# Attention and MLP on one core: transfers cut along other dimensions, first queries turned by TensorE, four chunks' residuals on ScalarE and GpSimd, and new instruction orders

## The chip, the core and the metric

The kernel runs on one core of a Trainium2 chip. Its time is the device time of one execution in microseconds (us). A core has five engines with a queue each, which run in order and wait for each other by semaphores: TensorE (PE; its weight loads are shown as PEld), VectorE (DVE), ScalarE (ACT), GpSimd (POOL) and SyncE (SP). Transfers are issued from the queues of SP and ACT here (one from POOL) and are moved by 16 DMA engines.

## What is computed

Two blocks follow each other. The first is attention with a polynomial sketch, without a softmax: with batch 4, 4 heads, 1088 tokens, head size 32 and r = 8,

```python
def phi(x):
    a = np.einsum('rd,bhsd->bhsr', S1, x)
    b = np.einsum('rd,bhsd->bhsr', S2, x)
    return np.einsum('bhsi,bhsj->bhsij', a, b).reshape(*x.shape[:-1], r * r)
q_p, k_p = (phi(q), phi(k))
kv = np.einsum('bhsf,bhsd->bhfd', k_p, v)
z = np.sum(k_p, axis=2)
num = np.einsum('bhsf,bhfd->bhsd', q_p, kv)
den = np.einsum('bhsf,bhf->bhs', q_p, z)[..., None] + 1e-06
attn = num / den
```

The heads are then put side by side, x of shape (4, 1088, 128), and the second block is

```python
xn = (x - mu) / np.sqrt(var + 1e-06) * g_ln
out = x + np.maximum(xn @ w_ch1, 0.0) @ w_ch2
```

with 512 hidden columns. S1, S2 and both weights come as float64; the kernel makes float32 of them with integer and float operations on their two words.

## The kernel before, in words

**Stages of a batch.** A batch's k and q are loaded (`ld`) and turned by DVE in blocks of 32 x 32 (`turn_g`, `turn_r`), so that head and feature lie on the partitions. For batch 0, `k_dir` and `q_dir` make the features on PE straight with tokens on the partitions; for the others `k_feat` and `q_feat` make them in packed 32-row matmuls and DVE turns them (`k_tok`, `q_tok`). `k_prod` and `q_prod` make the 64 products per token (POOL or DVE). `k_sum`, `k_zs`, `k_sc`, `k_sccp` give the denominator's vector, `k_val`, `k_vcp`, `k_spr`, `k_rcp` the value matrix. `q_ac`, `q_den`, `q_rec`, `q_a2` divide, `q_turn` turns the products, and `num` (PE) gives x, turned, in PSUM; `num_cp` and `num_r` copy it to SBUF.

**Chunks.** x is worked on in eight chunks of 512 tokens (0 to 7, two for each batch) and two of 128 (8 and 9, the last 64 tokens of two batches each). For a chunk, `hid` (PE, one of four blocks of hidden columns) and `relu` make the hidden layer, `sec` (PE, one of four 128-token tiles, 8 matmuls) the second product; the normalisation is put into w1 (`fold`) and, as a factor rstd, behind the second product. x itself is also needed with tokens on the partitions ("rows"): for mean and variance (`st_bn`, `st_ag`, then `st_pow` on POOL for the power -0.5) and for the residual. Chunks 0, 1, 8 and 9 get their rows by PE (`row_pe`, `row_cp`); chunks 2 to 7 by way of DRAM: `row_turn` on DVE, `row_wr` (a store to a scratch tile) and four `row_rd` (loads back, one for each head). `fin` (DVE) scales by rstd and adds the rows, into one of two buffers `ob`, and `store` sends the chunk.

**What sets the order.** Nothing is scheduled: a string `PROGRAM` lists the operations by name, engine letter (V, A, G, S) and arguments, and each engine gets its instructions in the order of this list. At most eight transfers of SP and ACT are under way together: their eight semaphores go round, and an issue waits for the eighth before it. PSUM has the banks X and Y (two tiles of 1024 columns each, for `num` and the features), M, N, O and K; `hid` uses M and N, `sec` mostly O.

**Lines.** `ld_v` 132-138, `ld_vr` 141, `row_turn` 692, `row_wr` 696, `row_rd` 701, `st_bn` 708, `st_ag` 713 (line 717 is the addition of 1e-6), `hid` 732, `relu` 738, `sec` 747, `fin` 761, `store` 782, `store_r` 791. Line 85 is the helper for elementwise products, line 80 that for ACT copies. The shapes of the transfers that the change touches are these (step and count of each dimension, DRAM side):

```python
# ld_v:   [[8 * D, 4], [G * D, 32], [1, 8 * D]]   into 128 partitions, one head
# row_wr: [[P, P], [P * P, 4], [1, P]]            from 128 partitions
# row_rd: [[P * P, 4], [P, 32], [1, P]]           into 128 partitions, one head
# store:  [[8 * DM, 4], [G * DM, 32], [1, 512]]   from 128 partitions
```

Of the kernel before, what the change touches and what calls it, by code (L numbers as in the profile page):

```python
# [25 lines left out]
def kernel(  # L26
# [44 lines left out]
    banks = {"X": XS[0], "Y": XS[1], "M": M[0], "N": M[1], "O": PO, "K": KV}  # L71
# [26 lines left out]
    qn = const([P, G * D], F32, "qn", B)  # L98
# [67 lines left out]
    mhalf = const([P, 4], F32, "mhalf")  # L166
    m896 = const([P, 1], F32, "m896")
# [249 lines left out]
    @op  # L417
    def turn_r(x, b):
        dst, src = turned[x]
        o = 1024 + 64 * (b % 2)  # L420
        dve.transpose(dst[b % 2][:, o : o + 64], src[b][:, 1024:1088])
# [8 lines left out]
    @op  # L430
    def k_dir(u0, u1, z):
        for u in range(u0, u1):
            pe.matmul(banks[z][:, KW * (u - u0) : KW * (u - u0 + 1)], kT[0][:, P * u : P * (u + 1)],
                      sk0, start=True, stop=True)
# [228 lines left out]
    xh = const([P, 512], F32, "xh", 2)  # L663
    xd = [dram.tile([P, 512], F32, name=f"xd{i}") for i in range(8)]
# [5 lines left out]
    obs = const([P, 512], F32, "ob", 2)  # L670
# [42 lines left out]
    def st_ag(c):  # L713
        n, st, mv = tiles(c), sts[slot(c)], mvs[slot(c)]
        for t in range(n):
            dve.bn_aggr(out=mv[:, 2 * t : 2 * t + 2], in_=st[:, 6 * t : 6 * t + 6])
        dve.tensor_scalar(out=vas[slot(c)][:, 0:n], in0=_ap(mv, 0, P, 1, [[2, n]]), scalar1=1e-6,  # L717
                          scalar2=None, op0=ALU.add)
# [42 lines left out]
    def fin(z, c, t):  # L761
        o, i0 = halves(c, obs[turn_of(c)][:, P * t : P * (t + 1)], banks[z][:, P * t : P * (t + 1)])
# [28 lines left out]
    def store_r(eng, c, i):
        b = 2 * (c - 8) + i
        by[eng].dma_start(
            out=bass.AP(out.tensor, out.offset + (b * S + 32) * DM,
                        [[DM, 2], [G * DM, 32], [1, DM]]),
            in_=obs[turn_of(c)][64 * i : 64 * i + 64, 0:P],
# [5 lines left out]
    ld_s A 0; ld_g; ld S k 0 0 16; c_small; c_ones; ld_s A 1; ld S k 0 16 34; c_iota;  # L802
    ld_u S q 0 0 4; c_act; c_pads 0; c_masks; ld_w S 1; c_vpad 3; c_vpad 2; ld_v S 0 0; c_rest;
    ld_v S 0 1; c_vpad 0; ld_v S 0 2; c_ac 0; c_vpad 1; w_ex V 0 0 64; c_ac 1; ld_v S 0 3;
    c_ident; w_exf V 0 0 64; w_e2 V 0 0 64; ld_vr S 0 0; w_bits V 0 0 64; turn_g k 0 0 2;
    w_mant A 0 0 64; c_pads 1; ld_vr S 0 1; w_addlow V 0 0 64; w_e3 V 0 0 64; s_heads V;
    turn_g k 0 2 4; fill 2 512; fill 1 256; sk; ld_u S q 0 4 8; turn_u q 0 0 4; sk_q; sk_2;
    sk_qq 2; sk_8; sk_0; sk_qq 3; sk_d; turn_r k 0; fill 1 256; fill 1 128; k_dir 0 3 X; c_cg V;
# [6 lines left out]
    q_dir 0 4 N; w_e3 V 1 0 256; ld_vr S 1 0; w_add G 1 256 512; turn_r q 0; turn_u q 0 4 8;
    k_val 0; w_e3 V 1 256 512; q_cp A 0 4 N 16 24; q_ac0 0 4 N 0; w_add G 1 0 256; q_den 0 0 4;
    q_rec 0 0 4; ld_vr S 1 1; w_low A 2 0 512; q_dir 4 9 O; w_mul G 1 0 256; q_b0 0 4 N 0;
    k_vcp A 0; q_prod0 0 2 N 0; w_mul G 1 256 512; q_prod0 2 4 N 0; k_spr 0; q_cp A 4 9 O 16 24;
    q_turn 0 2; k_rcp A 0; fold N 0 256; ld S k 2 0 34; turn_g k 1 0 4; num 0 0 2;
    fold_cp A N 0 256; turn_r k 1; num_cp A 0 0 0 2; q_turn 2 4; num_cp A 0 1 0 2; hid M 0 0 0 2;  # L820
    q_ac0 4 9 O 4; q_den 0 4 9; ld S q 2 0 34; hid N 0 1 0 2; q_rec 0 4 9; relu A M 0 0 0 2;
    turn_r q 1; ld_v S 2 0; num 0 2 4; q_b0 4 9 O 4; relu A N 0 1 0 2; q_prod0 4 9 O 4;
    ld_v S 2 1; fold M 256 512; ld_v S 2 2; num_cp A 0 1 2 4; num_cp A 0 0 2 4; ld_v S 2 3;
    row_pe 0 K; fold_cp A M 256 512; q_turn 4 9; ld_vr S 2 0; row_cp A 0 K; hid N 0 2 0 2;
    ld_vr S 2 1; hid M 0 3 0 2; relu A N 0 2 0 2; w_bits V 2 0 512; relu A M 0 3 0 2; num 0 4 9;
    turn_g q 1 0 4; w_mant A 2 0 512; ld S k 3 0 34; w_add G 2 0 512; hid M 0 1 2 4; turn_r k 2;
    num_r A 0; turn_g k 2 0 4; num_cp A 0 0 4 8; num_cp A 0 1 4 8; k_feat 1; relu A M 0 1 2 4;
    w_ex V 2 0 512; row_pe 1 K; ld S q 3 0 34; k_tok 1; w_exf A 2 0 512; hid M 0 3 2 4;
    ld_v S 3 0; turn_r q 2; row_cp A 1 K; k_prod G 1 5 9; w_e2 V 2 0 512; hid N 0 0 2 4;
    ld_v S 3 1; relu A M 0 3 2 4; st_bn 1; k_sum 1; relu A N 0 0 2 4; ld_v S 3 2; hid M 1 1 0 4;  # L830
    k_zs 1; turn_g q 2 0 4; ld_v S 3 3; ld_vr S 3 0; k_prod G 1 0 5; k_sc 1; ld_vr S 3 1;
    hid N 0 2 2 4; relu A M 1 1 0 4; k_sccp V 1; st_bn 0; q_feat 1; relu A N 0 2 2 4; st_ag 0;
    hid N 1 0 0 4; w_e3 V 2 0 512; k_val 1; st_pow 0; turn_r k 3; relu A N 1 0 0 4; q_tok 1 0;
    turn_g k 3 0 4; w_mul G 2 0 512; hid N 1 2 0 4; k_vcp A 1; turn_r q 3; q_tok 1 1; sec O 0 3;
    relu A N 1 2 0 4; q_ac V 1 0 4; q_den 1 0 4; sec O 0 2; q_ac V 1 4 9; q_rec 1 0 4; st_ag 1;
    q_a2 G 1 0 4; turn_g q 3 0 4; sec O 0 1; q_prod G 1 0 4; sec O 0 0; q_den 1 4 9; q_rec 1 4 9;
    hid M 1 3 0 4; fin O 0 0; fin O 0 1; q_a2 G 1 4 9; fin O 0 3; fin O 0 2; k_feat 2; q_turn 0 4;
# [76 lines left out]
```

## Time and profile before

| What | Value |
|---|---|
| Runs | 139.17, 141.32, 141.88 us; median 141.32 |
| Profiled execution, span | 139.2 us |
| Busy: PE, DVE, POOL, ACT | 105.5, 75.8, 49.4, 39.6 us |
| Mean granted TensorE clock | 0.89 |
| DMA | 13.32 MB in 14023 packets, mean 96 GB/s |

The profiled execution's span is taken by the profiler from the first to the last instruction. In the profile, a busy row gives the share of each of 40 equal slices in tenths (9 is 90% or more); the clock row gives the TensorE clock that was granted; the DMA row gives the mean busy share of the 16 DMA engines. A group or timeline row names line, engine, operation, output<-inputs, shape and count, and in brackets the idle time in front of it and what ended that. Matmul times overlap each other, since matmuls are pipelined.

### The profile page before, as it was taken

To read this page: it belongs to the slowest core of one execution; us is meant where nothing else is said; L and a number is where in the kernel's file an instruction comes from. 1 tells how busy PE (TensorE), PEld (TensorE's weight loads), DVE (VectorE), ACT (ScalarE), POOL (GpSimd) and SP (SyncE) were. 2 spreads that over 40 slices of the span, in tenths; PEclk is the share of its full clock that TensorE was granted. 3 is DMA by queue.
4 is the path that set the end of the run, shared out by engine and by line. 5 is a ranking of instruction groups with operands and counts; after the bars stand their busy time and mean duration, and the time that the engine had idled before them with its cause. 6 is when DMAs were issued, how large, how long until landed. Compare 5 with 4: busy or idle time off the path is not lost.

```text
span 139.2 us, 3266 instructions
## 1 busy us (share of the span) xinstructions
PE 105.5 (76%) x1336; PEld 72.0 (52%) x1336; DVE 75.8 (54%) x225; ACT 39.6 (28%) x99; POOL 49.4 (36%) x62
## 2 busy tenths in 40 slices
PE   5998598999986899999105999907999999970000
PEld 2486565764483865493003785403779467970000
DVE  4897499879599839400994307079434400038110
ACT  4055143486211132604200505104114443210000
POOL 6329300039917992610667600047800100005000
PEclk9999855699999999999975799996899999999555
DMA  4849939528532115223002052221002612210220
GB/s 137 238 132 227 315 111 245 158 101 235 177 99 68 16 64 151 57 79 77 24 0 56 19 153 66 78 87 26 0 0 37 196 30 66 82 49 0 36 102 31
DMA packets 14023, 13.32 MB, mean 96 GB/s; under 512 B 1848, under 2 KB 11832, under 8 KB 14008
## 3 DMA queue, kind: packets, MB, share of 16 engines
q1 hardware_dynamic: 13812, 13.04, 33.1%
q8 instruction: 10, 0.16, 0.5%
q10 hardware_dynamic: 164, 0.07, 0.2%
q14 instruction: 5, 0.04, 0.1%
q0 software_dynamic: 32, 0.00, 0.0%
HBM read 9.31 MB, written 3.80 MB: 94 GB/s over the span
## 4 chain that ended last, share of the span: by engine, by line
DMA 46%; SPq 16%; DVE 14%; PE 10%; POOL 4%; issue 3%; ACT 3%; DVEq 0%; ACTq 0%
DMA vn<-in_v_dram 15%; DMA x<-xd 12%; DMA xd<-xh 9%; SPq L702 9%; DMA kn<-in_k_dram 5%; DMA out_dram<-ob 4%; PE X L633 4%; SPq L133 3%; POOL qp L85 3%; DVE st L710 3%; PE M L734 3%; DVE qpT L619 3%; PE PO L750 3%; ACT xT L80 2%; DVE xh L693 2%
## 5 line engine op out<-in xcount | busy, mean ns | idle before, releaser
L734 PE MATMUL M<-xT,w 128*128 128x512 f32 (+1 forms) x72 | 34.8, 604 | 5.0 <-ACT hT L742 4.6
L742 ACT ACTIVATE hT<-M 128x512 f32<-128x512 f32 (+2 forms) x44 | 21.4, 500 | 36.5 <-PE M L734 30.1
L750 PEld LDWEIGHTS PO<-w,hT 128*128 128x128 f32 x208 | 25.1, 194 | 7.0 <-DVE ob L763 3.2
L750 PE MATMUL PO<-w,hT 128*128 128x128 f32 x208 | 26.4, 279 | 1.9 <-DVE ob L763 1.4
L723 POOL TENSOR_TENSOR rstd<-va,mhalf 128x4 f32<-128x4 f32 (+1 forms) x10 | 9.6, 957 | 48.7 <-DVE va L717 48.5
L710 DVE BATCH_NORM_STATS2 st<-x 128x6 f32<-128x128 f32 x32 | 7.0, 280 | 27.1 <-DMA x<-xd 27.0
L734 PEld LDWEIGHTS M<-xT,w 128*128 128x128 f32 x72 | 12.3, 201 | 15.2 <-ACT hT L742 10.3
L85 POOL TENSOR_TENSOR kp<-kf 128x1024 f32<-128x1024 f32 (+3 forms) x8 | 15.2, 1916 | 3.6 <-ACT kf L80 2.2
L85 POOL TENSOR_TENSOR qp<-a,fq 128x1024 f32<-128x1024 f32 (+1 forms) x6 | 13.0, 2171 | 0.4
L619 DVE STREAM_TRANSPOSE qpT<-qp 128x1280 f32<-128x1280 f32 (+2 forms) x9 | 11.1, 1228 | 2.5 <-POOL qp L85 2.4
L80 ACT COPY xT<-X 128x256 f32<-128x256 f32 (+1 forms) x18 | 5.4, 361 | 17.3 <-PE X L633 17.3
L633 PE MATMUL X<-qpT,kvr 32*32 32x288 f32 (+2 forms) x384 | 9.4, 404 | 0.3 <-DVE qpT L619 0.3
L750 PEld LDWEIGHTS X<-w,hT 128*128 128x128 f32 x64 | 7.8, 192 | 1.4 <-issue 1.4
L237 PE MATMUL M<-ones 128*128 128x256 f32 (+2 forms) x16 | 7.2, 574 | 1.5 <-DVE ones L181 1.5
L750 PE MATMUL X<-w,hT 128*128 128x128 f32 x64 | 8.0, 275 | 0.0
L475 PE MATMUL KV<-kf 128*32 128x32 f32 x72 | 1.7, 212 | 8.0 <-DVE kf L460 8.0
L763 DVE SCALAR_TENSOR_TENSOR ob<-PO,rstd,x 128x128 f32<-128x128 f32 x24 | 6.7, 337 | 1.8 <-PE PO L750 1.8
L633 PEld LDWEIGHTS X<-qpT,kvr 32*32 32x32 f32 x384 | 5.2, 119 | 3.6 <-issue 2.1
L305 POOL TENSOR_TENSOR mant<-mant,low 128x256 f32<-128x256 f32 (+1 forms) x3 | 2.9, 988 | 11.5 <-ACT mant L283 11.5
L581 DVE STREAM_TRANSPOSE fq<-X 128x576 f32<-128x576 f32 x6 | 4.4, 754 | 4.1 <-PE X L572 4.1
L504 PE MATMUL KV<-kp,vn 128*32 128x64 f32 x288 | 5.1, 221 | 1.2 <-DMA vn<-in_v_dram 1.1
L475 PEld LDWEIGHTS KV<-kf 128*32 128x32 f32 x72 | 1.2, 121 | 9.1 <-DVE kf L460 8.2
(115 smaller groups left out, 123.7 us busy)
## 6 DMA issues: line engine op xcount, KB each, us to landing
vn<-in_v_dram SPq DMA_DIRECT2D x16, 128.0 KB
out_dram<-ob SPq DMA_DIRECT2D x8, 256.0 KB
kn<-in_k_dram SPq DMA_DIRECT2D x3, 544.0 KB
qn<-in_q_dram SPq DMA_DIRECT2D x3, 544.0 KB
xd<-xh SPq DMA_DIRECT2D x6, 256.0 KB
x<-xd SPq DMA_DIRECT2D x24, 64.0 KB
w_raw<-in_moe_w_ch_dram SPq DMA_DIRECT2D x2, 512.0 KB
qn<-in_q_dram SPq DMA_DIRECT2D x2, 256.0 KB
```

The source lines that it names most:

```text
L80: act.copy(o, i)
L85: by[eng].tensor_tensor(out=o, in0=a, in1=b, op=ALU.mult)
L237: pe.matmul(M[0][:, 0:w], ones[:, 0:P], ones[:, 0:w], start=True, stop=True)
L619: dve.transpose(_ap(qpT, 0, P, 32 * u0, [[32, u1 - u0], [TW, 8], [1, 32]]), qp[:, H * F * u0 : H * F * u1])
L633: pe.matmul(XS[r // 2][D * h : D * h + D, o : o + w], kvr[b % 2][rows, DM * f + D * h : DM * f + D * h + D], qpT[rows, c : c + w], start=( ...
L702: by[eng].dma_start(out=rows_of(c)[:, P * h : P * (h + 1)], in_=bass.AP(xd[c].tensor, xd[c].offset + 32 * P * h, [[P * P, 4], [P, 32], [1, ...
L710: dve.bn_stats(out=sts[slot(c)][:, 6 * t : 6 * t + 6], in_=row_ap(c, t))
L723: pool.tensor_tensor(out=rstds[slot(c)][:, 0:n], in0=vas[slot(c)][:, 0:n], in1=mhalf[:, 0:n], op=ALU.pow)
L734: pe.matmul(banks[z][:, 0:n], w1[:, P * j : P * (j + 1)], cols(c)[:, a : a + n], start=True, stop=True)
L742: act.activation(o, i, AF.Relu)
L750: pe.matmul(banks[z][:, DM * t : DM * (t + 1)], h[:, 512 * j + P * t : 512 * j + P * (t + 1)], w2[:, DM * j : DM * (j + 1)], start=(j == 0 ...
L763: dve.scalar_tensor_tensor(out=o, in0=i0, scalar=rstds[slot(c)][:, t : t + 1], in1=row_ap(c, t), op0=ALU.mult, op1=ALU.add)
```

## The change

What it does:

1. **Transfers with 32 or 128 outer runs.** `ld_v` takes all heads of 32 partitions (8 tokens each) in place of one head in all 128; `row_wr` and `row_rd` write and read a chunk whole, with 128 runs, one read in place of four; `store` has 128 runs for batch 0 and 32 x 4 for the others. To fit, `num_cp`, `row_turn` and `turn_r` place the tokens in another order, and w1 and w2 are loaded in parts.
2. **First queries.** Batch 0's q is loaded with tokens on the partitions (`ld_t`, `ld_tr`: pieces of 32 floats, 128 bytes) and turned by PE (`turn_p`, nine transposes) and copied by ACT (`turn_c`), in place of `ld_u` and DVE's `turn_u`.
3. **Residuals.** Chunks 0, 1, 2 and 3 use `fin_a` (ACT scales the product by rstd into `ob`) and `fin_g` (POOL adds the rows) in place of `fin`. There are four `ob` buffers in place of two.
4. **Smaller ones.** Batch 1's k uses `k_dir` as batch 0 does. The 1e-6 in `st_ag` comes from a tile (`tensor_tensor`) in place of a constant (`tensor_scalar`). The halves of X and Y are banks of their own (A to D), and `hid` and `sec` use all of them. Some relus, PSUM copies, products and all of w2's unpacking but one step are on DVE.
5. **Orders.** The list `PROGRAM` is another one. Rows of chunks 4 and 5 are read from ACT's queue (`row_rd A 5`, `row_rd A 4`, behind `relu A D 4 3`), the others from SP's; chunk 7 goes to DRAM and back ahead of chunk 6; in front of the first `num` now stand both batches' `k_dir` and `k_feat 2`; k is loaded from ACT's queue first.

The core of the diff:

```diff
+             "A": XS[0][:, 0:512], "B": XS[0][:, 512:1024],
+             "C": XS[1][:, 0:512], "D": XS[1][:, 512:1024]}
...
-    def ld_v(eng, b, h):
-            out=vn[b][:, TW * h : TW * h + 8 * D],
-                        [[8 * D, 4], [G * D, 32], [1, 8 * D]]),
+    def ld_v(eng, b, g):
+        by[eng].dma_start(out=_ap(vn[b], 32 * g, 32, 0, [[TW, H], [1, 8 * D]]),
+                                      [[G * D, 32], [S * D, H], [1, 8 * D]]))
...
+    def ld_t(eng, h, u0, u1):
+            in_=bass.AP(q.tensor, q.offset + (h * S + u0) * D, [[8 * D, P], [D, u1 - u0], [1, D]]),
...
+    def turn_p(z, u0, u1):
+            pe.transpose(banks[z][:, P * (u - u0) : P * (u - u0) + n],
+                         qt[0:n, P * u : P * (u + 1)], ident[0:n, 0:n])
+    def turn_c(eng, z, u0, u1):
+        copy(eng, qT[0][:, P * u0 : P * u0 + n], banks[z][:, 0:n])
...
-        by[eng].dma_start(out=bass.AP(xd[c].tensor, xd[c].offset, [[P, P], [P * P, 4], [1, P]]),
-                          in_=xh[c % 2].rearrange("p (r w) -> p r w", r=4))
+        by[eng].dma_start(out=bass.AP(xd[c].tensor, xd[c].offset, [[w, P], [1, w]]),
+                          in_=xh[slot(c)])
...
-    def row_rd(eng, c, h):
-            in_=bass.AP(xd[c].tensor, xd[c].offset + 32 * P * h, [[P * P, 4], [P, 32], [1, P]]),
+    def row_rd(eng, c):
+            in_=bass.AP(xd[c].tensor, xd[c].offset, [[w, P], [P * w, H], [1, w]]),
...
-        dve.tensor_scalar(out=vas[slot(c)][:, 0:n], in0=_ap(mv, 0, P, 1, [[2, n]]), scalar1=1e-6,
-                          scalar2=None, op0=ALU.add)
+        dve.tensor_tensor(out=vas[slot(c)][:, 0:n], in0=_ap(mv, 0, P, 1, [[2, n]]),
+                          in1=eps[:, 0:n], op=ALU.add)
...
-    obs = const([P, 512], F32, "ob", 2)
+    obs = const([P, 512], F32, "ob", 4)
...
-                        [[8 * DM, 4], [G * DM, 32], [1, 512]]),
-            in_=obs[turn_of(c)],
+        runs = [[8 * DM, P]] if b == 0 else [[G * DM, 32], [8 * DM, 4]]
+                        runs + [[1, DM * (t1 - t0)]]),
+            in_=ob(c)[:, DM * t0 : DM * t1],
...
-    ld_s A 0; ld_g; ld S k 0 0 16; c_small; c_ones; ld_s A 1; ld S k 0 16 34; c_iota;
+    c_ones; fill 1 128; ld_g; ld_s S 1; c_pads 1; c_small; c_pads 0; c_vpad 1; c_iota; c_ident;
```

The rest of the list is new in the same manner.

More of the change, by code (lines that the diff above doesn't have):

```diff
@@ L803 @@
[L803 to L808, printed above, removed]
@@ L815 @@
[L815 to L820, printed above, removed]
@@ L821 @@
[L821 to L837, printed above, removed]
-    q_prod G 1 4 9; relu A M 1 3 0 4; store S 0; sec O 1 0; k_tok 2; sec O 1 1; k_prod G 2 5 9;
@@ L839 @@
-    q_turn 4 9; k_spr 1; sec O 1 2; k_rcp A 1; k_sum 2; num 1 0 9; k_prod G 2 0 5; k_zs 2; k_sc 2;
-    num_cp A 1 1 4 8; sec O 1 3; num_cp A 1 1 0 4; k_sccp V 2; num_cp A 1 0 0 4; st_pow 1;
-    num_r A 1; num_cp A 1 0 4 8; row_turn 2; k_val 2; row_turn 3; row_wr S 2; fin O 1 0;
-    row_wr S 3; fin O 1 3; q_feat 2; fin O 1 2; k_vcp A 2; fin O 1 1; store S 1; hid N 2 0 0 4;
-    q_tok 2 0; q_tok 2 1; row_rd S 2 3; hid M 2 1 0 4; relu A N 2 0 0 4; row_rd S 2 0;
-    q_ac V 2 0 4; row_rd S 2 2; hid N 2 2 0 4; q_den 2 0 4; relu A M 2 1 0 4; q_rec 2 0 4;
@@ L851 @@
-    st_bn 8; st_ag 8; k_tok 3; st_pow 8; hid M 3 3 0 4; relu A N 3 2 0 4; k_prod G 3 0 5;
-    hid N 8 0 0 1; relu A M 3 3 0 4; k_sum 3; num 2 0 9; relu A N 8 0 0 1; k_zs 3; k_prod G 3 5 9;
-    hid N 8 2 0 1; num_cp A 2 1 0 4; num_cp A 2 1 4 8; k_sc 3; sec O 3 3; relu A N 8 2 0 1;
-    k_sccp V 3; num_cp A 2 0 4 8; num_cp A 2 0 0 4; row_turn 5; num_r A 2; hid M 8 1 0 1;
-    sec O 3 0; row_turn 4; relu A M 8 1 0 1; row_wr S 5; hid N 4 0 0 4; row_wr S 4; sec O 3 2;
-    k_val 3; row_rd S 5 1; row_rd S 5 2; q_feat 3; row_rd S 5 3; k_vcp A 3; row_rd S 4 2;
@@ new lines @@
+    turn_g k 3 0 4; turn_r k 3; num_r V 1; num_cp A 1 1 4 8; num_cp A 1 1 0 4; ld_v A 3 3;
+    turn_r q 2; num_cp V 1 0 0 4; num_cp V 1 0 4 8; row_turn 2; row_turn 3; turn_r q 3; st_ag 0;
+    sec N 0 2; sec M 1 3; k_feat 3; k_tok 3; sec M 1 0; hid C 2 1 0 4; k_sum 3; hid O 2 2 0 4;
+    sec M 1 2; row_wr S 3; st_pow 0; fin_a N 0; relu A C 2 1 0 4; row_wr A 2; row_rd S 3;
+    row_rd S 2; fin_g G 0; relu A O 2 2 0 4; turn_g q 2 0 4; turn_g q 3 0 4; k_zs 3; q_feat 2;
+    hid N 3 0 0 4; sec M 1 1; k_spr 2; q_tok 2 1; q_tok 2 0; st_bn 1; st_ag 1; k_prod G 3 0 5;
@@ new lines @@
+    relu A D 4 3 0 4; q_prod G 3 4 9; q_a2 G 3 0 4; fin_g G 3; row_turn 5; row_wr S 4; row_wr S 5;
+    sec K 8 0; hid O 5 3 0 4; hid C 4 1 0 4; hid B 5 1 0 4; hid N 4 0 0 4; row_pe 8 A;
+    hid D 5 2 0 4; row_rd A 5; st_pow 2; row_rd A 4; q_prod V 3 0 4; q_turn 4 9; k_rcp A 3;
+    q_turn 0 4; row_cp V 8 A; st_bn 5; fin_a M 2; relu A O 5 3 0 4; fin_g G 2; relu A B 5 1 0 4;
+    relu A N 4 0 0 4; relu A C 4 1 0 4; hid M 5 0 0 4; relu A M 5 0 0 4; relu A D 5 2 0 4; st_ag 5;
+    st_bn 8; st_bn 4; st_ag 4; st_pow 4; sec K 4 2; sec K 4 1; num 3 0 9; fin K 4 1;
@@ new lines @@
+    num_cp V 3 0 4 8; num_cp A 3 1 0 4; store A 2 0 4; num_r A 3; num_cp A 3 1 4 8; sec N 4 0;
+    sec M 5 2; st_ag 8; fin N 4 0; num_cp A 3 0 0 4; st_pow 8; st_pow 5; store S 3 0 4;
+    store S 0 0 4; row_turn 6; row_turn 7; row_wr S 7; row_rd S 7; row_pe 9 D; sec D 5 1;
+    sec N 4 3; fin N 4 3; row_cp V 9 D; hid C 6 1 0 4; st_bn 9; hid B 6 3 0 4; hid N 7 2 0 4;
+    relu V B 6 3 0 4; sec D 5 0; fin M 5 2; fin D 5 0; fin K 4 2; fin K 8 0; relu V C 6 1 0 4;
+    row_wr S 6; hid A 6 0 0 4; hid O 9 0 0 1; sec M 5 3; hid C 7 0 0 4; relu A A 6 0 0 4;
```

177 lines of the change are left out of this document (112 added, 65 removed).

## The prediction

> **What bounds the kernel now.** I read the page first: busy shares, the 40 slices, granted clock, DMA share.
>
> ```profile
> PE 105.5 (76%) x1336; PEld 72.0 (52%) x1336; DVE 75.8 (54%) x225; ACT 39.6 (28%) x99; POOL 49.4 (36%) x62
> PE   5998598999986899999105999907999999970000
> PEclk9999855699999999999975799996899999999555
> DMA  4849939528532115223002052221002612210220
> ```
>
> TensorE (PE) is the busiest engine, but its row shows where it was stopped: slices 19 to 21, 26 and 27, and the last four or five. A slice is 3.48 us. The list of waits and the timelines around these stops say who made it stop (times are from the span's start).
>
> ```profile
> PE KV L475 <- DVE kf L460: 8.0, 1, 8.0
> PE M L734 <- ACT hT L742: 4.6, 1, 4.6
> PE PO L750 <- DVE ob L763: 1.4, 1, 1.4
> DVE st L710 <- DMA x<-xd: 27.0, 4, 14.5
> ```
>
> ```profile
> 66.00 0.87 DVE L710 BATCH_NORM_STATS2 st<-x 128x6 f32<-128x128 f32 x4 [8.41 <-DMA x<-xd]
> ...
> 69.78 1.03 DVE L717 TENSOR_SCALAR va<-mv 128x4 f32<-128x4 f32 x1
> ...
> 73.76 0.77 DVE L460 STREAM_TRANSPOSE kf<-X 128x576 f32<-128x576 f32 x1
> ```
>
> ```profile
> 123.46 1.06 PE L750 MATMUL PO<-w,hT 128*128 128x128 f32 x8
> ...
> 134.32 0.35 DVE L763 SCALAR_TENSOR_TENSOR ob<-PO,rstd,xr 128x128 f32<-128x128 f32 x1 [5.00 <-DMA out_dram<-ob]
> 134.70 0.53 SPq L793 DMA_DIRECT2D out_dram<-ob  x1
> ```
>
> The last matmul ends at 123.46 + 1.06 = 124.52. All three stops have one cause: rows of x sent through DRAM come back late. VectorE (DVE) stands 8.41 us in front of `st_bn 2`, and the `k_tok 3` that PE waits for is queued behind it (73.76). At the end the rows arrive as PE finishes, and the last `fin` waits 5.00 us more for an `ob` buffer whose store is under way. The stretches table tells why the rows are slow (columns: stretch, length, busy time of PE, PEld, DVE, ACT, POOL, granted clock, DMA share, GB/s).
>
> ```profile
> 57.00:66.00 9.00, 9.00 (x62) 5.56 (x60) 0.56 (x3) 3.50 (x7) 2.57 (x3) 1.00 0.28 76
> 80.40:82.40 2.00, 2.00 (x27) 1.40 (x30) 0.00 (x0) 0.00 (x0) 0.00 (x0) 1.00 0.94 262
> 83.00:91.00 8.00, 7.19 (x89) 4.02 (x77) 2.98 (x8) 2.67 (x6) 0.00 (x0) 1.00 0.25 69
> 112.00:125.00 13.00, 12.52 (x88) 10.43 (x86) 1.03 (x8) 3.79 (x9) 0.00 (x0) 1.00 0.24 61
> ```
>
> While rows of x are read (57 to 66, 83 to 91, 112 to 125) the share is 0.24 to 0.28, about 4 of 16 DMA engines, at 61 to 76 GB/s. `row_rd` has 4 outer runs. While `row_wr`, with 128, moves (80.4 to 82.4), 0.94 of the engines run at 262 GB/s. A busy share of a quarter for a shape with a 4 in front is the key to the change.
>
> **The change, part by part**, against the profiled execution: its span is 139.2, which is also the lowest of the three runs (139.17; median 141.32, 1.5% above).
>
> (1) Rows of x, both directions. One chunk is 256 KB: 256/69 = 3.8 us of movement on 4 engines, 256/262 = 1.0 on all. What a round trip takes beside that, the chain of waits bounds.
>
> ```profile
> 52.75 4.03 DMA xd<-xh
> 59.30 6.57 DMA x<-xd
> 106.12 4.82 DMA xd<-xh
> ```
>
> A pair of writes is back after 4.0 to 4.8 us, of which 2.0 is movement; so one transfer takes 2.4 to 4, and I take 3.0, nearer the first since one write moves half as much. A chunk's trip is write 3.0, issue 0.5, read 3.0: 6.5 us, where before the reads of a pair alone took 6.57 from their last issue. What covers it is what the program puts between `row_turn 3` and `st_bn 3` on DVE.
>
> ```profile
> L581 DVE STREAM_TRANSPOSE fq<-X 128x576 f32<-128x576 f32 x6 | 4.4, 754 | 4.1 <-PE X L572 4.1
> ...
> L404 DVE STREAM_TRANSPOSE qT<-qn 128x1024 f32<-128x1024 f32 x3 | 3.7, 1232 | 0.0
> ```
>
> `turn_g q 2` and `turn_g q 3` are 2.4, `k_tok 3` and two `q_tok` 2.3, `st_bn 1` 0.9, and a relu of 512 columns, `st_ag` twice and small ones some 2.4: about 8 us. SP and ACT carry one write each there, so the second row lands some 7.5 us after the turns. Hidden by 0.5; if that cover is gone, the price is the 4.6 or 8.0 of before, less the 3 saved. So both stops go: **-8.0 and -4.6**. With `through_dram` rows 4 and 5 the reads are issued by ScalarE (ACT), which stands in them until the write has landed: its relus wait some 2 us, and PE has five `hid` into other PSUM banks in that time; in (5).
>
> (2) The end. Four `ob` buffers and 16-engine stores take away the 5.00. After the third batch's `num`, PE has 15 `sec` and 8 large `hid` left (a `sec` is the row at 123.46, at most 1.06, and a `hid` is as many products: 21 to 24 us); the trips of chunks 7 and 6 go one after the other on SP, 2 x 6.5, with copies, turns, statistics and pow 5 more: 18 us, under 21 to 24. So PE's end should set the end: one `fin` 0.35, issue 0.5 and 139.2 - 134.70 = 4.5 from there, 5.4 behind PE instead of 14.7: **-9.3**. With 4 us per transfer the rows come 3 us too late; that is in the range.
>
> (3) The clock.
>
> ```profile
> 16.60:20.50 3.90, 3.88 (x14) 2.88 (x14) 3.76 (x9) 1.59 (x4) 0.73 (x1) 0.50 0.38 147
> 20.50:26.80 6.30, 5.91 (x138) 4.24 (x138) 6.16 (x12) 2.38 (x8) 0.00 (x0) 0.50 0.80 213
> 71.20:78.00 6.80, 3.41 (x84) 1.86 (x85) 3.45 (x9) 0.32 (x2) 4.64 (x4) 0.50 0.15 39
> 95.10:98.50 3.40, 3.40 (x7) 1.46 (x6) 2.48 (x4) 0.91 (x3) 2.66 (x3) 0.50 0.08 20
> ```
>
> Half clock follows each stop. The last two stretches hold 3.41 and 3.40 us of PE at half speed: with their stops gone, **-3.4**. The first (9.8 us of PE at half) comes from thin work at the start, which stays thin; I keep it, and its 4.9 us is the range's lower reserve. The Trainium skill, "TensorE: Matmul & The Clock Gate", Part 1, says that the clock falls to half after an idle window of about 3.4 us and returns after a busy one; the stops of 8.0 and 4.6 agree, and by it alone the sum would be the same here. The 1.4 for PO goes too (more banks for `hid` and `sec`): **-1.4**. Together 139.2 - 8.0 - 4.6 - 9.3 - 3.4 - 1.4 = 112.5.
>
> (4) The start and PE's added work.
>
> ```profile
> L451 PE MATMUL X<-kT,sk 64*32 64x288 f32 x48 | 2.1, 415 | 0.0
> ...
> L475 PE MATMUL KV<-kf 128*32 128x32 f32 x72 | 1.7, 212 | 8.0 <-DVE kf L460 8.0
> ...
> L684 PE MATMUL KV<-ident,xT 128*128 128x128 f32 x8 | 1.6, 335 | 0.0
> L433 PE MATMUL X<-sk,kT 128*128 128x64 f32 x12 | 1.6, 279 | 0.0
> ...
> L80 ACT COPY xr<-KV 128x128 f32<-128x128 f32 x2 | 0.5, 266 | 2.4 <-PE KV L684 2.4
> ```
>
> Nine `turn_p` at 1.6/8 = 0.2 are 1.8; nine `k_dir` of batch 1 (two matmuls each, 1.6/6 = 0.27) are 2.4 in place of one `k_feat`, 2.1/3 = 0.7: PE gets 3.5 more. In front of the first `num` now stand all of these, `k_feat 2` (0.7) and two `k_sum` (1.7/4 = 0.42 each): 5.7 us of PE that needn't be done later.
>
> ```profile
> 15.64 0.24 DVE L421 STREAM_TRANSPOSE qT<-qn 128x64 f32<-128x64 f32 x1 [2.50 <-DMA qn<-in_q_dram]
> 16.70 0.28 DVE L85 TENSOR_TENSOR ac<-M,fq 128x128 f32<-128x128 f32 x1
> ```
>
> ```profile
> 20.52 1.10 PE L633 MATMUL X<-qpT,kvr 32*32 32x64 f32 x64
> ```
>
> On DVE, `sk_0` comes about 1.1 us later (two weight operations stand ahead of the k transposes, `s_heads` is on POOL), then four k transposes that before ran later; but the 2.50 us wait for q is gone. I put `q_ac0` at 16 to 18 and the first `num` at 22.5 instead of 20.5: +2.0, bounds 0 and +5 (the latter with all 5.7 us of added PE work in line). Net 2.0 + 3.5 - 5.7 = **-0.2**. First queries in pieces of 128 bytes make more and smaller packets; their price isn't shown in before by itself, between 0 (they land while k is transposed) and the 2.5 that q's wait cost. I take 0, for `turn_p` stands behind eighteen matmuls.
>
> (5) What is new on the other engines. Four chunks' `fin` go from DVE (4 x 0.3) to ACT (4 copies at 0.27, 1.1 us) and a POOL addition of 512 elements; DVE gets relus and PSUM copies instead, some 5 us net. Between the second and the third `num` I count, by the group table's durations, some 20.6 us of DVE work against 23.0 of PE (estimates), in long chains with POOL products between: thin cover. How DVE fares beside POOL is seen in two rows.
>
> ```profile
> 68.40 2.39 POOL L85 TENSOR_TENSOR qp<-a,fq 128x1280 f32<-128x1280 f32 x1
> ...
> 69.78 1.03 DVE L717 TENSOR_SCALAR va<-mv 128x4 f32<-128x4 f32 x1
> ```
>
> ```profile
> L717 DVE TENSOR_SCALAR va<-mv x10: 153/170/1460, 35.2 to 126.8; 128x4 f32<-128x4 f32 x8, 128x1 f32<-128x1 f32 x2
> L300 DVE SCALAR_TENSOR_TENSOR bits<-w_raw,ex x3: 383/678/943, 12.2 to 36.0; 128x256 uint32<-128x256 uint32 x2, 128x512 uint32<-128x512 uint32 x1
> ```
>
> An operation of 0.17 us took 1.03 and ended at 70.81, just when POOL's product (68.40 + 2.39 = 70.79) did: it stood behind GpSimd. So each DVE operation of that kind may cost up to 2.4. The change gives `va` a second input in place of the constant, and moves all of w2's unpacking, two products and several copies to DVE beside POOL. Bounds: 0 (PE is ahead and never notices) to 12 (five such waits reach PE). I take 2, plus 1 for ACT's stand before `row_rd`, plus 1 for a fresh half-clock window: **+4.0**.
>
> Sum: 112.5 - 0.2 + 4.0 = 116.3. The median stood up to 1.5% above the profiled run; I predict **117**.
>
> **Rivals.** (A) DVE and POOL take turns often enough that PE is fed late: four or five more of these waits, 2.0 each, and another half-clock window: 117 + 10 = 127. For it: the two rows above and 20.6 against 23.0; against: both engines have spare time elsewhere. The Trainium skill, "SBUF — State Buffer", section "SBUF: two separate sides", says that GpSimd and VectorE share a pair of ports under an exclusive lock, taken by VectorE operations with two SBUF inputs as well as by the two-port kinds; by it the new `va` escapes nothing. The 943 ns of L300, which has two inputs, against 383 for the same shape agrees. (B) The transfers do not spread: reads stay at 69 GB/s, 2.8 us more per chunk, three pairs; about 1 + 4 + 4 us reach PE's path: 126. Against it: the 0.94 of `row_wr`. (C) All goes well: the first half-clock stretch shrinks too and (5) costs nothing: 112.3 - 4.9 = 107. (D) Slower: DVE and POOL in turns all through. Busy 75.8 + 49.4, plus the 2 net that both change by, plus about 16 in which DVE must wait for PE or the ends: 143 to 146. It decides from the point where over 24 us of POOL's time is handed on to PE, half its busy time; in before 69.78 is the rare case.
>
> **Chances.** About 117 (110 to 123): 0.60. C: 0.14. A and B together (123 to 136): 0.16. Within 2% of before, A at its worst: 0.04. D: 0.06. Range 107 to 128: the likeliest case, C and most of A and B. A measurement of this kernel can tell about 2% from no change; faster by more 0.90, same 0.04, slower 0.06.
>
> **What would show it.** The DMA share near 0.9 in short bursts while rows are read; no DVE wait of over 3 us for `x<-xd`; no PE stop of over 3 us after 30; PE's last matmul about 5 to 6 us before the end; first `num` piece at 22 to 23; half clock nowhere after 30. Wrong if DVE rows beside POOL become several times longer than alone and PE waits name DVE, if ACT's relus stand behind `row_rd`, or if the first `num` comes after 26.

## The result, and the profile after

| Kernel | Median, us | Runs |
|---|---|---|
| before | 140.93 | 139.17 to 141.88 |
| changed | 122.68 | 122.64 to 123.15 |

The ratio is 0.883 (95% interval 0.878 to 0.889). The profiled execution took 122.71 us, its span is 120.9. Predicted were 117 for the time and, as the sum for the span, 116.3: the direction is right, the time is 5.7 and the span 4.6 above the forecast. In the experiments below some kernels also have executions several per cent longer than their shortest; medians and ranges there are over all executions. The page of the changed kernel (busy line, then slices of 3.02 us):

```profile
PE 108.4 (90%) x1347; PEld 78.6 (65%) x1347; DVE 84.0 (69%) x229; ACT 38.7 (32%) x100; POOL 48.4 (40%) x64
PE   5993999999898998998999799999979979979970
PEclk9999999999999999999999999999999999999997
DMA  3999799996000023011640120013640225300423
```

The stops of 8.0 and 4.6 us and most of the tail are gone. PE's busy time has *grown* from 105.5 to 108.4. Two stretches in which rows of x are read, and the end:

```profile
58.00:61.00 3.00, 3.00 (x43) 1.74 (x44) 1.99 (x4) 2.08 (x6) 1.82 (x2) 1.00 0.58 175
84.60:88.00 3.40, 2.89 (x9) 1.05 (x7) 3.40 (x3) 1.67 (x6) 2.14 (x3) 1.00 0.66 199
```

```profile
116.18 1.06 PE L788 MATMUL X<-w,hT 128*128 128x128 f32 x8
...
117.33 0.35 DVE L801 SCALAR_TENSOR_TENSOR ob<-X,rstd,xr 128x128 f32<-128x128 f32 x1 [0.60 <-PE X L788]
117.71 0.55 SPq L833 DMA_DIRECT2D out_dram<-ob  x1
```

The DMA share is 0.58 and 0.66, against 0.24 to 0.28 before. These are means over stretches that also hold issue and latency, and other transfers too: a row write and a load of v in the first, two stores in the second. PE's last matmul ends at 117.24, and the end comes 3.7 behind it instead of 14.7. The start is where the forecast failed. First ScalarE's queue, then VectorE and PE (start, duration, engine; in brackets the idle time before):

```profile
1.68 2.21 ACTq L118 DMA_DIRECT2D kn<-in_k_dram  x2
6.06 0.39 ACTq L150 DMA_DIRECT2D qt<-in_q_dram  x1
6.48 1.28 ACT L206 ACT_TABLE_LOAD   x1 [6.48 <-DMA qt<-in_q_dram]
...
9.92 0.41 ACTq L150 DMA_DIRECT2D qt<-in_q_dram  x1
10.38 0.43 ACT L308 ACTIVATE low<-w_raw 128x256 f32<-128x256 uint32 x1 [2.00 <-DMA kn<-in_k_dram]
10.71 0.16 ACT L408 COPY skq<-KV 128x16 f32<-128x16 f32 x1
```

```profile
11.14 0.22 DVE L380 TENSOR_TENSOR sk<-KV,m 128x64 f32<-128x64 f32 x1
```

```profile
7.05 2.50 PE L254 MATMUL M<-ones 128*128 128x128 f32 x6
11.41 1.54 PE L463 MATMUL X<-sk,kT 128*128 128x64 f32 x6 [1.86 <-DVE sk L380]
...
17.01 1.49 PE L463 MATMUL X<-sk,kT 128*128 128x64 f32 x6
...
31.58 0.84 PE L663 MATMUL X<-qpT,kvr 32*32 32x64 f32 x64 [0.42 <-ACT fq L82]
```

ScalarE is free after 3.9, but each `ld_t` in its queue has to wait until one of the eight transfers under way has landed (the bracket at 10.38 names a load of k), and `sk_q` stands behind them until 10.71. VectorE's `sk_8` and `sk_0` wait for it, PE stands 1.86 us, and the first `num` comes at 31.58, not at 22.5. Six matmuls of `k_dir` take 1.49 us. Before:

```profile
9.35 0.83 PE L433 MATMUL PO<-sk,kT 128*128 128x64 f32 x6
```

The same work takes 1.8 times as long. That is half clock, though the clock row says 1.0: run 1 below has the same 1.49 us beside a recorded clock of 0.50. The weight loads of the fills (`fill`: matmuls on ones that only keep PE busy), which are the same work in both kernels, say it too (minimum, median, maximum in ns; after, then before):

```profile
L254 PEld LDWEIGHTS M<-ones x16: 286/333/337, 1.4 to 21.5; 128*128 128x128 f32 x16
```

```profile
L237 PEld LDWEIGHTS M<-ones x16: 186/192/337, 1.5 to 11.8; 128*128 128x128 f32 x16
```

### The profile page after: what moved, and what is told of

It is laid out like the page before. It is cut to its first block, busy times and chain, and to the rows that moved or that the text cites. A ratio compares the mean times of both kernels' runs of the same rounds, so it can differ in the third digit from the quotient of the medians.

```text
span 120.9 us, 3295 instructions
## 1 busy us (share of the span) xinstructions
PE 108.4 (90%) x1347; PEld 78.6 (65%) x1347; DVE 84.0 (69%) x229; ACT 38.7 (32%) x100; POOL 48.4 (40%) x64
## 4 chain that ended last, share of the span: by engine, by line
PE 57%; DVE 18%; DMA 8%; ACT 6%; issue 4%; POOL 2%; ACTq 1%; DVEq 0%; POOLq 0%
PE X L772 8%; PE M L788 7%; PE X L663 5%; PE M L772 5%; DMA kn<-in_k_dram 4%; PE X L788 4%; DVE xh L725 4%; PE KV L788 3%; PE X L463 3%; DVE qpT L649 3%; DMA w_raw<-in_moe_w_ch_dram 3%; PE PO L788 3%; PE PO L772 2%; ACT xT L82 2%; PE M L463 2%
## 5 line engine op out<-in xcount | busy, mean ns | idle before, releaser
L758 POOL TENSOR_TENSOR rstd<-va,mhalf 128x4 f32<-128x4 f32 (+1 forms) x10 | 10.2, 1024 | 29.1 <-DVE va L752 28.1
L788 PEld LDWEIGHTS M<-w,hT 128*128 128x128 f32 x144 | 17.1, 192 | 5.1 <-issue 2.4
L788 PE MATMUL M<-w,hT 128*128 128x128 f32 x144 | 18.4, 278 | 1.1 <-ACT ob L807 0.6
L772 PE MATMUL X<-xT,w 128*128 128x512 f32 (+1 forms) x38 | 18.4, 586 | 0.8 <-DVE xr L84 0.8
L780 ACT ACTIVATE hT<-X 128x512 f32<-128x512 f32 (+2 forms) x18 | 9.9, 556 | 21.3 <-PE X L772 19.8
L87 POOL TENSOR_TENSOR kp<-kf 128x1280 f32<-128x1280 f32 (+3 forms) x7 | 13.1, 1883 | 4.9 <-ACT kf L82 3.2
L87 POOL TENSOR_TENSOR qp<-a,fq 128x1280 f32<-128x1280 f32 (+1 forms) x4 | 9.6, 2398 | 5.1 <-DVE a L87 5.0
L772 PE MATMUL M<-xT,w 128*128 128x512 f32 (+1 forms) x20 | 9.0, 532 | 1.4 <-DVE hT L782 0.9
L254 PE MATMUL M<-ones 128*128 128x128 f32 (+2 forms) x16 | 8.7, 696 | 1.4 <-DVE m L202 1.4
L725 DVE STREAM_TRANSPOSE xh<-xT 128x512 f32<-128x512 f32 x6 | 6.5, 1102 | 0.9 <-ACT xT L82 0.9
L772 PEld LDWEIGHTS M<-xT,w 128*128 128x128 f32 x20 | 3.4, 189 | 5.5 <-issue 1.9
```

The lines of the kernel that those rows point to most:

```text
L87: by[eng].tensor_tensor(out=o, in0=a, in1=b, op=ALU.mult)
L254: pe.matmul(M[0][:, 0:w], ones[:, 0:P], ones[:, 0:w], start=True, stop=True)
L725: dve.transpose(_ap(xh[slot(c)], 0, P, 0, [[32 * n, 4], [32, n], [1, 32]]), _ap(cols(c), 0, P, 0, [[1, 4], [P, n], [4, 32]]))
L758: pool.tensor_tensor(out=rstds[slot(c)][:, 0:n], in0=vas[slot(c)][:, 0:n], in1=mhalf[:, 0:n], op=ALU.pow)
L772: pe.matmul(banks[z][:, 0:n], w1[:, P * j : P * (j + 1)], cols(c)[:, a : a + n], start=True, stop=True)
L780: act.activation(o, i, AF.Relu)
```

## The experiments

Twelve kernels ran; every time is a median with its range, beside runs of before at 139.9 to 141.0 in the median.

**1. Is it the clock alone?**

```diff
-    fill 1 128; fill 1 256; fill 1 256; k_dir 0 3 6 C; ...
+    fill 3 512; k_dir 0 3 6 C; ...
```

> The changed kernel with three fills of 512 columns between `sk` and the first `k_dir`, in place of 128, 256 and 256. Theory (the late first `num` comes from half clock: in the changed kernel every weight load of a fill takes 0.29 to 0.34 us from 1.4 to 21.5, while before most take 0.19): PE goes to full clock before `k_dir`, the 14.6 us of PE work from 11.4 to 26 shrink by 5 or more against some 1 to 2 us of added fill, the first `num` comes at 26 to 28 instead of 31.6, and the time is 117 to 120. Rival (the late `num` hangs on data, on VectorE's and ScalarE's orders, not on the clock): the fills only push `k_dir` back, first `num` at 32 to 34, time 123 to 125.

Measured: 122.69 (122.43 to 123.33), no gain; the first `num` comes at 30.06, between what the theory and the rival said. The longer fill did run at full clock (1536 columns in 2.84 us, where 640 took 2.50 in the changed kernel), but PE then stood 1.85 us for `sk_0` as in the changed kernel, and half clock was back soon after:

```profile
14.00:20.00 6.00, 6.00 (x45) 5.82 (x45) 2.72 (x6) 2.28 (x7) 3.00 (x8) 0.50 0.95 206
```

```profile
6.71 2.84 PE L254 MATMUL M<-ones 128*128 128x512 f32 x6
11.40 0.88 PE L463 MATMUL X<-sk,kT 128*128 128x64 f32 x6 [1.85 <-DVE sk L380]
...
12.79 1.40 PE L463 MATMUL M<-sk,kT 128*128 128x64 f32 x6
...
15.68 1.49 PE L463 MATMUL X<-sk,kT 128*128 128x64 f32 x6
```

Here the clock row has 0.50, and the same `k_dir` take the same 1.49 us as in the changed kernel, whose row has 1.00: the record, not the clock, differed. What follows: the fill ahead of this stop was lost, so the stop has to go.

**2. Is it ScalarE's queue?** The two `ld_t` that ScalarE issued go to SP, behind its own two.

```diff
-    ... ld A k 1 0 34; ld_t A 2 0 4; ld_tr S; ...
-    ld_t A 3 0 4; w_low A 1 256 512; ld_t S 0 0 4; ld_t S 1 0 4; ...
+    ... ld A k 1 0 34; ld_tr S; ...
+    w_low A 1 256 512; ld_t S 0 0 4; ld_t S 1 0 4; ld_t S 2 0 4; ld_t S 3 0 4; ...
```

> The changed kernel with the two `ld_t` that ScalarE issues in the head moved to SP's queue, behind its own two. Theory (ScalarE stood in these issues, so that `sk_q` came at 10.7 and `sk_0` at 11.1): `sk_q` at 7 to 8, `sk_0` at 8 to 9, the first `k_dir` at 9.6 where the fills end; if half clock stays, first `num` at 29.5 to 30 and the time 120.5 to 121.5. Rival (the late `sk_0` is not on the path, since the second batch's k lands at 10.4 and the first queries at 13 or later): first `num` at 31 to 32, time 122 to 123.5.

Measured: 117.68 (115.36 to 120.72), more than expected; the profiled execution (115.89, span 114.1) shows why:

```profile
6.71 0.17 ACT L408 COPY skq<-KV 128x16 f32<-128x16 f32 x1 [0.60 <-PE KV L376]
```

```profile
6.61 1.35 PE L254 MATMUL M<-ones 128*128 128x128 f32 x6
8.17 0.88 PE L463 MATMUL X<-sk,kT 128*128 128x64 f32 x6 [0.21 <-DVE sk L380]
...
11.48 0.83 PE L463 MATMUL X<-sk,kT 128*128 128x64 f32 x6
...
21.72 0.84 PE L663 MATMUL X<-qpT,kvr 32*32 32x64 f32 x64 [0.42 <-ACT fq L82]
```

`sk_q` comes 4.0 earlier, PE's stop is 0.21 instead of 1.86, full clock holds through `k_dir` (0.83), and the first `num` is at 21.72: 9.9 earlier from two moved issues. The stop itself is 1.65 of this; `k_dir` starts 3.2 earlier, and the other 6.6 are the same matmuls at full clock. PE's busy time falls from 108.4 to 101.6 for the same instructions, so half clock cost the changed kernel at least 6.8: run 2 has some of its own, behind a stop of 1.89 at 27.5 (clock 0.55 from 29.6 to 33.4). The fills ahead of the stop already ran at half clock in the changed kernel (2.50 us; here 1.35), so there the stop didn't end full clock but kept it from coming; that a stop also ends it is run 1's. The times spread over 5 us from execution to execution.

**3. What were narrow transfers worth?** The changed kernel with the transfers of before (four reads per chunk, 4 outer runs; stores of batches 1 to 3 with 4 outer runs; `row_wr`, `num_cp` and `row_turn` place the tokens as before to fit):

```diff
-    [[w, P], [P * w, H], [1, w]]            # row_rd, one
+    [[P * P, 4], [P, 32], [1, P]]           # row_rd, four, all on SP
...
-    [[G * DM, 32], [8 * DM, 4]] + ...       # store
+    [[8 * DM, 4], [G * DM, 32]] + ...
```

> The changed kernel with the row transfers of before: four reads of a quarter each (all on SP), with 4 outer runs, and the results of batches 1 to 3 stored with 4 outer runs; order, buffers and all else as changed. Theory (4 of 16 engines were the cause of the stops): reads go at 60 to 80 GB/s, VectorE waits over 3 us for rows of x, PE stops several us, time 131 to 141. Rival (the new orders give the rows so much time that width does not matter): time 122.5 to 126.

Measured: 133.53 (133.24 to 134.65), 10.9 more than the changed kernel, in the theory's range. Two rows of its list of waits (us in total, times, longest us):

```profile
DVE st L745 <- DMA x<-xd: 9.1, 3, 4.4
...
DVE ob L801 <- DMA out_dram<-ob: 5.1, 1, 5.1
```

Both waits of before are back, in the new order and with four buffers: narrow transfers, not the order or the number of buffers, had made them. Runs 4 and 5 below, with two buffers and wide stores of batches 1 to 3, have no wait for a store in their lists.

**4 and 5. Transfers alone.** The kernel before with one wide read per chunk and wide writes and stores; orders, buffers, queries and residuals as before. Run 4 stores the first batch's two chunks with 128 outer runs, which puts their tokens into the wrong rows of the output and leaves some rows unwritten, while the bytes moved are the same; run 5 leaves these two stores at 4 runs. Both have the new `row_wr`, `row_rd`, `row_turn` and `num_cp`, which are not shown.

```diff
...
-    [[8 * DM, 4], [G * DM, 32], [1, 512]]                            # store, all
+    [[8 * DM, P]] if b == 0 else [[G * DM, 32], [8 * DM, 4]] ...     # run 4
+    [[8 * DM, 4], [G * DM, 32]] if b == 0 else ...                   # run 5
```

> The kernel before with the wide transfers alone: rows of x written and read as 128 outer runs, one read per chunk where its first read stood, results of batches 1 to 3 stored with 32 outer runs; order, two result buffers, queries and residuals as before. Theory (the transfers alone carry most of the gain): the stops of 8.0 and 4.6 us shrink to 3 or less and the end shortens by some 5; time 124 to 131. Rival (the orders carry it): 135 to 140.

> The kernel before with the wide transfers alone, as in the run before this one, which stored the first batch's chunks to the rows of another order; here the first batch's two chunks keep their 4 outer runs and their place, batches 1 to 3 are stored with 32 outer runs. Theory (the transfers alone carry the whole gain, since that run took 120.6): 119.5 to 122. Rival (part of that run's gain came from the first batch's stores): 124 to 130.

Measured: 120.62 (119.90 to 121.25), better than the theory said, and 127.53 (126.55 to 127.95), the rival's range. Two narrow stores of 256 KB cost 6.9 us. The store of chunk 1 is issued between the writes and the reads of chunks 2 and 3; run 4, then run 5, SP's queue and VectorE:

```profile
55.26 0.34 SPq L786 DMA_DIRECT2D out_dram<-ob  x1
56.05 1.04 SPq L704 DMA_DIRECT2D x<-xd  x2
```

```profile
59.10 0.87 DVE L712 BATCH_NORM_STATS2 st<-x 128x6 f32<-128x128 f32 x4 [0.69 <-DMA x<-xd]
```

```profile
57.12 0.57 SPq L786 DMA_DIRECT2D out_dram<-ob  x1
57.81 1.03 SPq L704 DMA_DIRECT2D x<-xd  x2
```

```profile
65.45 0.87 DVE L712 BATCH_NORM_STATS2 st<-x 128x6 f32<-128x128 f32 x4 [5.19 <-DMA x<-xd]
```

The same wide reads give their rows 3.1 us after their issue in run 4 and 7.6 after it in run 5, where the DMA share from 61 to 65 is 0.34: that they wait for engines which the narrow store still holds is argued from this order, as the profile names no engine. And `k_tok 3`, queued behind, stops PE for 6.3 again. So the transfers alone carry a gain as large as the whole change's, 20 us in run 4, if *all* are wide; the store of batch 0 can be wide only with its tokens in another order, which goes with `ld_t` and `turn_p`. The rest of the change gave nothing net; with its head mended (runs 2, 11 and 12) it gives 3 to 5 us in the median.

**6 to 8. Buffers and residuals.**

```diff
-    obs = const([P, 512], F32, "ob", 4)
+    obs = const([P, 512], F32, "ob", 2)             # run 6
-    fin_a N 0; ... fin_g G 0;                       # also chunks 1, 2, 3
+    fin N 0 0; fin N 0 1; fin N 0 2; fin N 0 3;     # run 7 at fin_g's place, run 8 at fin_a's
```

> The changed kernel with two result buffers instead of four. Theory (the fourth buffer is needed: the 5.00 us in front of the last `fin` before): VectorE's or ScalarE's residuals wait for stores 2.9 us long again, time 124 to 128. Rival (with wide stores two buffers come free in time): 122.5 to 123.5.

> The changed kernel with four residuals per chunk on VectorE for chunks 0 to 3 too (at the place of the GpSimd additions), none on ScalarE and GpSimd. Theory (VectorE is a thin cover, moving them away was needed): 4.8 us more on VectorE reach PE in part, time 124 to 127. Rival (PE alone is the bound, and the four GpSimd additions of 1.28 us slow VectorE as much as they relieve it): 121.5 to 123.

> The changed kernel with the residuals of chunks 0 to 3 on VectorE, now at the place where ScalarE's copies stood (the run before put them behind the next products in the same bank, so they read other sums); no copy on ScalarE, no addition on GpSimd. Theory (VectorE is a thin cover between the second and the last `num`, 4.8 us more on it reach PE in part): 123.5 to 127. Rival (PE alone is the bound and GpSimd's additions cost VectorE as much as they take off it): 121.5 to 123.

Measured: 124.52 (124.12 to 125.56), 127.17 (125.67 to 128.24), 125.10 (123.42 to 127.00). Run 6 is no clean test: the new order stores chunk 0 after chunk 2 has been put into the same buffer, so some rows that it stores are another chunk's. Run 7 read banks that already held other products. Run 8 is the test of the residuals. With them on VectorE the kernel is slower by 2.4 in the median, but its range begins only 0.8 above the changed kernel's. The profiled execution is 1.5 slower, and one row carries that (PE, run 8):

```profile
90.68 1.12 PE L772 MATMUL M<-xT,w 128*128 128x512 f32 x2 [3.26 <-DVE ob L801]
```

The changed kernel has a wait of 0.51 there, at 87.91; the next `num` comes 1.6 later than in it, at 93.52.

**9. Is PE's work the bound in the head?** Batch 1's features by `k_feat` and `k_tok` instead of nine `k_dir` and three copies.

```diff
-    k_dir 1 3 6 M; k_dir 1 0 3 D; ... k_dir 1 6 9 A; k_cp A 1 3 6 M; ...
+    k_feat 1; ... k_tok 1;
```

> The changed kernel with batch 1's features of k made as before, by one `k_feat` and a `k_tok` on VectorE, in place of nine `k_dir` and three ScalarE copies. Theory (PE is the bound all through, so PE work counts in full): PE has 1.7 us less at full clock and up to 3.4 less at half, the first `num` comes 2 to 3.5 us earlier and the time is 119 to 120.7. Rival (`k_tok` on VectorE and the later data hold the head, or half clock returns elsewhere): 122 to 123.

Measured: 122.80 (121.83 to 124.77): the rival's time, and for the second of its two reasons, since half clock returned. `k_tok` and the data didn't hold the head: the first `num` comes at 26.74, 4.8 earlier, and the last piece of batch 0's `num` at 40.42, 0.6 earlier. In between PE stopped 1.07 and 1.74 us with nothing but "issue" named, and behind the second stop matmuls took 1.06 us for 0.60 again.

**10 to 12. Can the head be mended?** All three with the moved `ld_t`. Run 10 also takes the loads of q for batches 2 and 3 out of the first 31 us, run 12 has two fills of 512 columns ahead of `k_dir`, run 11 both.

```diff
-    ... ld S q 3 0 34; ... ld S q 2 0 34; ...
+    ... ld A k 3 0 34; ld A q 2 0 34; ld A q 3 0 34; ...     # runs 10, 11
-    fill 1 128; fill 1 256; fill 1 256; k_dir 0 3 6 C; ...
+    fill 2 512; k_dir 0 3 6 C; ...                           # runs 11, 12
```

> The run with ScalarE's two loads moved to SP, and beside that the loads of q for batches 2 and 3 (544 KB each) taken out of the first 31 us and issued by ScalarE behind its load of k for batch 3, at about 36. Theory (PE's stop of 1.89 us at 27.5, ended by nothing but the arrival of instructions, is instruction traffic queued behind full data transfers: two instruction packets moved in 25 to 31 at a busy share over 0.9): the stop falls under 1 us, no half clock after it, time 112 to 114.5 in the best runs. Rival (the stop is a fixed latency of the fetch, whatever the load): a stop of 1.7 to 2 stays, time 115 to 116 in the best runs.

> The same as the run named here before it (late q), and two fills of 512 columns between `sk` and the first `k_dir` in place of 128, 256 and 256. Theory (the two levels of the times with the moved queue, 115.4 to 115.9 and 119.5 to 120.7, are executions with and without full clock in the head; a longer fill keeps it): all executions within 1.5 us of each other, at 113 to 115.5. Rival (the levels have another cause): spread of 4 to 5 us stays, and the best time is up to 0.9 longer.

> ScalarE's two loads moved to SP and the two fills of 512 columns, with the loads of q where the change had put them. Theory (half clock in the head makes the upper level): all executions at 115.5 to 117. Rival: spread of 115.5 to 121 stays.

Measured: 116.88 (116.52 to 121.00), 115.51 (113.35 to 121.90), 115.84 (113.19 to 119.53). The best executions of runs 11 and 12 come down to 113.2 to 113.6, but a spread of 4.5 us or more stays in all three. The theory that the longer fills end the spread fell; what makes the spread isn't shown, as each run has one profile. The theory that PE's stop of 1.89 at 27.5 in run 2 is instruction traffic behind full data transfers isn't borne out either: with the loads of q moved the stop did fall to 0.5 (run 10), but it is 0.45 in the changed kernel with them in place, and run 1 has a stop of 1.95 at the same place in the program, with the transfers at rest:

```profile
38.02 0.30 PE L663 MATMUL X<-qpT,kvr 32*32 32x64 f32 x3 [1.95 <-issue]
```

```profile
36.00:38.00 2.00, 0.07 (x8) 0.00 (x0) 1.97 (x2) 0.27 (x1) 2.00 (x2) 1.00 0.00 0
```

This stop always stands among the last matmuls of `num 0 2 4`: 0.45 us in the changed kernel, 0.5 in run 10, 0.8 in 11, 1.2 in 12, 1.74 in run 9, which has two more (0.76 and 1.07) elsewhere. What sets its length stays open. Runs 11 and 12 are the fastest kernels here, some 7 us under the changed one in the median; they don't differ by more than their spread.

The rows at which `num` starts tell all of this in one table (us, from the timelines):

| Kernel | first `num` | `num 0 4 9` | `num 1` | last `sec` | span |
|---|---|---|---|---|---|
| changed | 31.58 | 41.05 | 50.96 | 116.18 | 120.9 |
| run 1 | 30.06 | 41.26 | 51.09 | 116.26 | 121.0 |
| run 9 | 26.74 | 40.42 | 50.13 | 115.31 | 120.1 |
| run 10 | 25.69 | 35.25 | 45.08 | 110.27 | 115.0 |
| run 11 | 23.94 | 33.75 | 43.57 | 108.75 | 113.5 |
| run 2 | 21.72 | 34.30 | 44.12 | 109.31 | 114.1 |
| run 12 | 21.56 | 33.47 | 43.05 | 108.24 | 113.1 |

From `num 1` to the last `sec` every one of them takes 65.2. What is won in the head arrives in full, unless a stop ahead of `num 0 4 9`, and the half clock behind it, takes it back. Runs 11 and 12 have no stop ahead of `k_dir`, and both run it at full clock, although run 11 comes to it from fills at half clock (1024 columns in 3.78 us, 1.98 in run 12).

## Why the prediction was right in direction and 4.6 short

In terms of PE, the predicted 116.3 were 105.6 busy (105.5 - 3.4 + 3.5) and 10.7 idle; measured are 108.4 and 12.5. The missing 4.6 us of span are 2.8 busy (steps 3 and 4) and 1.8 idle: 4.1 more in front of the first `num`, less 1.7 at the end and 0.6 between. The prediction named the first `num` after 26 as a sign of being wrong, and that sign came. The other two came in part (a DVE row beside POOL took five times as long, ACT stood in `row_rd`), but at the small cost that step 5 gives.

- **Step 1, rows of x: right.** Both stops are gone, no `st_bn` waits for rows (idle 0.0), and a trip is 2.3 + 2.7 from issue to landing (rows below: count, size, median us) instead of the 3.0 + 3.0 assumed. Runs 3 to 5 show that it was the width. What the step didn't see is that wide reads issued behind a narrow store come late as well (runs 4 and 5).

```profile
xd<-xh SPq DMA_DIRECT2D x5, 256.0 KB, 2.3
...
x<-xd SPq DMA_DIRECT2D x4, 256.0 KB, 2.7
```

- **Step 2, the end: right,** 3.7 behind PE for 5.4. Run 3 gives the 5.1 us wait for `ob` back with four buffers, and runs 4 and 5 are without it with two, so the wide stores removed it rather than the buffers.
- **Step 3, clock: half right.** Nothing shows half clock after 30: weight loads from 33 on take 186 to 192 ns. But the first stretch, "kept" at 4.9, became at least 6.8 (108.4 - 101.6).
- **Step 4, the start: this is the term that failed.** "+2.0, bounds 0 and +5" for the first `num` is +11.1. The 22.5 was right for a head with full clock and a free ScalarE (run 2: 21.72). The sum had priced the new `ld_t` by when they land (0 to 2.5), but not by where they are issued: two of them stood in ScalarE's queue ahead of `sk_q`, 4.0 us, and with the stop of 1.86 behind that `k_dir` stayed at half clock. PE's added work is at most 4.4 for 3.5 (101.6, less 105.5 - 3.4 - 4.9 = 97.2), as 101.6 has run 2's own half clock in it. The prediction also didn't agree with itself here: with 3.3 us of PE idle in front of the first `num` before, + 2.0 for the later `num` and - 5.7 for work put in front leave -0.4 of idle, so 22.5 couldn't be had together with the half clock that step 3 keeps. Measured were 3.7 of idle.
- **Step 5, new waits: right in size.** PE is idle for 5.1 us between the first `num` and the last `sec`; the sum allowed 4.0 beside some 1.7 that before had there (33.7 idle less the stops, the end and 3.3 in the head). No new half-clock window came. ACT's stand in `row_rd A` is there, and PE waits 0.51 and 0.66 for ACT behind it:

```profile
84.56 0.95 ACTq L737 DMA_DIRECT2D x<-xd  x2
85.55 0.37 ACT L82 COPY kvr<-KV 128x256 f32<-128x256 f32 x1 [2.33 <-issue]
```

```profile
87.91 1.12 PE L772 MATMUL M<-xT,w 128*128 128x512 f32 x2 [0.51 <-ACT ob L807]
...
89.69 2.32 PE L788 MATMUL KV<-w,hT 128*128 128x128 f32 x16 [0.66 <-ACT hT L780]
```

  DVE behind POOL is there as well: the same operation alone, and beside a POOL product that ends at 30.53.

```profile
19.22 0.41 DVE L317 SCALAR_TENSOR_TENSOR bits<-w_raw,ex 128x256 uint32<-128x256 uint32 x1
...
28.59 1.94 POOL L87 TENSOR_TENSOR kp<-kf 128x1024 f32<-128x1024 f32 x1 [1.53 <-PE KV L534]
28.73 2.08 DVE L317 SCALAR_TENSOR_TENSOR bits<-w_raw,ex 128x256 uint32<-128x256 uint32 x1
```

  The Trainium skill, "SBUF — State Buffer", section "SBUF: two separate sides", calls this an exclusive lock that operations with two SBUF inputs also take; 2.08 for 0.41, ending at 30.81, agrees. It didn't reach PE: rival A (127) and D didn't come, as PE's waits for DVE after 31 are 0.9 at most.

B (narrow transfers after all) would have been 133.5 by run 3, not 126. C's mechanism, a first stretch at full clock, is there from `k_dir` to the first `num` in the profiled executions of runs 11 and 12; these took 115.3 and 114.8, and the best of both kernels 113.2, not 107.

## What to carry over

Transfers with 4 outer runs kept the DMA engines busy for about a quarter here (0.24 to 0.28), and wide reads issued behind a narrow store came 7.6 us after their issue for 3.1: make all of them wide. An issue is an instruction of its engine: in this program it waits, with eight transfers under way, for one to land, and so does what the engine has to compute behind it. Early in a kernel, price a stop of PE by the clock that it can lose (here 6.8 us beside a stop of 1.9), and read the clock from the times of equal matmuls as well as from its row.

## Unexpected behaviour of the hardware

- The clock record missed half clock: 1.00 all through the changed kernel's head, where weight loads take 333 ns and `k_dir` 1.49 us, as in run 1 with 0.50.
- Narrow work didn't bring full clock back. PE was dense from 11.4 on, and half clock lasted until about 27; in run 1 it went after a stop of 1.85, in run 10 around one of 0.70. The Trainium skill, "TensorE: Matmul & The Clock Gate", Part 1, gives an idle window of about 3.4 us for the fall and a busy one for the return. The stops here are shorter than that, and some 15 us of dense matmuls, many of them of 64 columns, passed before it was back; with fewer of them it was back earlier (run 9, about 19). That the window runs freely, as the Trainium skill says there, would fit the spread of runs 2 and 10 to 12, which no run here shows directly.
- A DVE transpose that reads with a step of four elements takes 1.10 us where the same tile read straight took 0.69 (rows below, after and before; 1102 and 690 are ns). Run 3, which reads straight and writes as the changed kernel does, has 0.70. No wait of PE names it here.

```profile
L725 DVE STREAM_TRANSPOSE xh<-xT 128x512 f32<-128x512 f32 x6 | 6.5, 1102 | 0.9 <-ACT xT L82 0.9
```

```profile
L693 DVE STREAM_TRANSPOSE xh<-xT 128x512 f32<-128x512 f32 x6 | 3.9, 690 | 2.0 <-ACT xT L80 2.0
```
